# Scores on 64 rows: odd elements of q and k placed beside the even ones by SBUF to SBUF copies, and an earlier request of the values that are summed in fours

## The chip, the cores and the metric

The kernel runs on one core of a Trainium2 chip. The metric is the device time of one execution in microseconds (us), read as the median of several runs. The profile is one execution taken by the hardware profiler; its span is some 2 us shorter than the device time, and its times count from the start of the span. TensorE is the matmul engine (PE in the profile; PEld is its weight load), VectorE is DVE, ScalarE is ACT, GpSimd is POOL, and SyncE is SP. SPq and POOLq are the DMA requests that those engines issue.

A run is called slow when it lies over 1.5% above the fastest run of the same kernel.

## The reference, cut to what matters

There are 8 batches, 8 heads, 576 positions and 64 elements per head. Every head gets two attentions, which are added: one over means of four positions (144 by 144), and one over neighbours less than four positions away. Then a feed-forward layer with two large matrices follows.

```python
q_d = q.reshape(B, H, 144, 4, D).mean(axis=3)        # k_d, v_d alike
out_up = repeat(softmax(q_d @ k_d.T / 8) @ v_d, 4)   # "pooled" part
mask = abs(pos[:, None] - pos[None, :]) < 4
out_local = softmax(where(mask, q @ k.T / 8, -1e9)) @ v
x = (out_up + out_local), laid out as 4608 tokens of 512
h = x @ w_in                                          # 512 -> 2048
out = (h * sigmoid(1.702 * h)) @ w_out                # 2048 -> 512
```

## The kernel before

The kernel works in nine groups of 512 tokens. Group g does the two large products of its tokens, 64 matmuls of 128x512 each, and the attention of batch g+1 is threaded between them at fixed steps: scores of the first half of the heads at step 13, of the second half at 33, the four products with the values (AV) at 42 to 53, transposes at 62 and 71. So the attention of batches 2 to 7, which the change touches, runs in groups 1 to 6. I call those six "the groups" below.

The kernel views two elements (bf16) that lie side by side as one 32-bit word and lets VectorE transpose the words (STREAM_TRANSPOSE in the profile, 1.24 to 1.25 us for 128x576 of them). By the kernel's indices, a head's 64 elements then lie on 32 partitions, an even and an odd one (index `a`) beside each other. So a score needs two matmuls of 32 rows each, one for `a = 0` and one for `a = 1`:

```python
def prep_1(name, b, qd):
    tt = work.tile([128, S, 2], BF16, name=f"{name}T{qd}", ..., bufs=1)
    t32 = tt.rearrange("p t a -> p (t a)").bitcast(FP32)
    nc.vector.transpose(out=t32..., in_=store[b, qd].bitcast(FP32)...)
    dst[b, qd] = tt

def scores(b, qd, barred=False):
    sp = [ps_tile(), ps_tile()]
    for i in range(5):
        for a in range(2):
            for par in range(2):
                for r in range(4):
                    rows = slice(32 * r, 32 * r + 32)
                    nc.tensor.matmul(
                        sp[r // 2][64 * par : 64 * par + 64, r % 2, 60 * i : 60 * i + 60],
                        lhsT=kT[b, qd][rows, k0 : k0 + 64, a],
                        rhs=qT[b, qd][rows, q0 : q0 + 60, a],
                        start=(a == 0 ...), stop=(a == 1 ...),
                        tile_position=(32 * r, 64 * par), ...)
```

`scores_d` does the same for the pooled scores, from `kdT` and `qdT`, which GpSimd makes in `pool_qk`. GpSimd takes its work in the order of the program, as its timeline below shows (103.98 to 122.06 us). The order per group is:

```python
        elif b < B:
            if b > 2:
                load_v4(b)               # SyncE requests v in fours
            prep_qk(b, 0)                # VectorE: transposes of the first half
            pool_qk(b, 0)                # GpSimd: kdT and qdT of the first half
            if b + 1 < B:
                for qd in range(NQ):
                    load_qk(b + 1, qd)   # GpSimd requests q, k of the next batch (4 DMAs)
            prep_v(b, nc.gpsimd)         # GpSimd: v to bf16
            if b + 1 < B:
                load_v(b + 1)
            prep_qk(b, 1)                # VectorE: transposes of the second half
            pool_qk(b, 1)                # GpSimd: kdT and qdT of the second half
            prep_v4(b, nc.gpsimd)        # GpSimd: sums of four values -> vd
```

AV multiplies first with `vb` (local part) and then with `vd` (pooled part), so it wants the last item of GpSimd's list.

The softmax here doesn't subtract the row's maximum and nothing guards it: scores larger than these inputs give would overflow.

## Time and profile before

| | before |
|---|---|
| device time, median of the first 3 runs | 331.39 us (331.34 to 332.75) |
| span of the profile | 329.5 us |
| TensorE busy, mean granted clock | 93%, 0.995 |
| matmuls in the trace | 4987 |
| time of one group (2 to 6) | 33.4 to 34.3 us, TensorE busy 32.5 to 32.8 us of it |

The page of the kernel before: the busy time of each engine, TensorE's granted clock in 40 slices (9 is 90% or more of full speed), and the engines' shares of the chain of work that ended last.

```profile
span 329.5 us, 11220 instructions
...
PE 308.0 (93%) x4987; PEld 157.9 (48%) x5043; DVE 130.2 (40%) x215; ACT 184.1 (56%) x322; POOL 138.9 (42%) x168
...
PEclk9997999999999999999999999999999999999999
...
PE 87%; issue 4%; SPq 3%; ACT 2%; DVE 2%; DMA 1%; DVEq 0%; ACTq 0%
```

TensorE is the bound: 87% of the chain is its own work, and its mean granted clock is 1.00 from 31 us on (0.94 before that).

The second of the six groups, by the view of windows. The columns are the stretch, its length, then each engine's busy time and instructions (PE, PEld, DVE, ACT, POOL), the TensorE clock, the DMA share and GB/s:

```profile
102.20:135.90 33.70, 32.79 (x595) 16.90 (x601) 16.33 (x25) 20.95 (x36) 17.52 (x19) 1.00 0.68 142
```

GpSimd in the same group, from the timeline (start, length, engine, line, operation, output and inputs, and in brackets the idle time before it and what ended it):

```profile
103.98 1.15 POOL L276 TENSOR_TENSOR pq<-kT 128x576 f32<-128x576 bf16 x1 [15.95 <-DVE kT L260]
...
105.83 1.15 POOL L276 TENSOR_TENSOR pq<-qT 128x576 f32<-128x576 bf16 x1
...
109.80 2.36 POOL L291 CAST vb<-vf 128x2560 bf16<-128x2560 f32 x1
...
113.97 1.15 POOL L276 TENSOR_TENSOR pq<-qT 128x576 f32<-128x576 bf16 x1
...
121.22 0.84 POOL L300 TENSOR_TENSOR vd<-v 112x256 bf16<-112x256 f32 x1
```

It starts when the first transpose is done and then has no gap until 122.06. TensorE in that stretch (`pa` and `pm` are its accumulators; `es` and `ed` are the exponentials of the local and the pooled scores):

```profile
113.50 0.84 PE L351 MATMUL pa<-qT,kT 32*64 32x60 bf16 x80
114.14 0.59 PE L370 MATMUL pa<-qdT,kdT 32*64 32x144 bf16 x24
114.66 2.76 PE L618 MATMUL pm<-xT,w_in_bf 128*128 128x512 bf16 x11
...
121.87 0.58 PE L370 MATMUL pa<-qdT,kdT 32*64 32x144 bf16 x24
...
124.43 0.35 PE L409 MATMUL pa<-vb,es 64*64 64x65 bf16 x20
124.61 0.32 PE L431 MATMUL pa<-vd,ed 48*64 48x65 bf16 x17
```

A score stage, 80 local and 24 pooled matmuls, takes from 113.50 to 114.66, 1.16 us. The pooled scores of the second half come at 121.87, and qdT was ready at 115.86. AV comes to `vd` at 124.61, and its ninth product with `vd`, at 124.68, is the first that needs the last sums. They were ready 2.6 us earlier. That 2.6 us is the slack that the change has to live with.

### The profile page before, as it was taken

Reading aid. Unit: us, or ns where it says so; the run is one execution under the profiler, and the core shown is the slowest. Engines: PE = TensorE matmul, PEld = TensorE weight load, DVE = VectorE, ACT = ScalarE, POOL = GpSimd, SP = SyncE. Lnnn points to the kernel's source line nnn. Section 1 sums busy time; section 2 is a strip of 40 time slices with the busy share of each in tenths; the row PEclk is TensorE's granted clock in tenths of the full one; section 3 lists DMA queues with packets and bytes.
Section 4 is the critical chain, followed back from the end, with each engine's and each line's share of the span. In section 5 each row is a group of like instructions: output and inputs, shape, how many; then the busy total and the mean of one; then the engine's idle time right before and its main releaser. Section 6 shows DMA issues by size and latency. Waiting matters only on the chain.

```text
span 329.5 us, 11220 instructions
## 1 busy us (share of the span) xinstructions
PE 308.0 (93%) x4987; PEld 157.9 (48%) x5043; DVE 130.2 (40%) x215; ACT 184.1 (56%) x322; POOL 138.9 (42%) x168
## 2 busy tenths in 40 slices
PE   8767999789999999999999999998999999999995
PEld 3444455445554455455544555455444544444444
DVE  4870512770468036802771277225730560000000
ACT  2552773375936683667367746674566646415611
POOL 7890844049603970298029901990098000000000
PEclk9997999999999999999999999999999999999999
DMA  7999979999814991398339922993180110011011
GB/s 126 184 188 208 171 151 183 196 210 236 191 39 132 205 207 39 116 193 171 102 100 200 200 83 86 196 195 105 40 172 2 60 41 32 2 72 56 2 62 65
DMA packets 63552, 41.36 MB, mean 126 GB/s; under 512 B 44048, under 2 KB 54416, under 8 KB 63504
## 3 DMA queue, kind: packets, MB, share of 16 engines
q1 hardware_dynamic: 55056, 26.95, 35.8%
q0 software_dynamic: 8304, 13.63, 23.9%
q8 instruction: 39, 0.64, 0.9%
q14 instruction: 9, 0.07, 0.1%
q10 hardware_dynamic: 144, 0.07, 0.1%
HBM read 44.83 MB, written 9.44 MB: 165 GB/s over the span
## 4 chain that ended last, share of the span: by engine, by line
PE 87%; issue 4%; SPq 3%; ACT 2%; DVE 2%; DMA 1%; DVEq 0%; ACTq 0%
PE pm L618 35%; PE pm L674 33%; PE pa L351 3%; SPq L214 3%; PE pa L618 2%; PE pa L431 2%; PE pa L409 2%; PE pa L370 2%; PE pa L458 2%; PE pa L674 2%; DMA vf<-in_v_dram 1%; PE pm L689 1%; PE pa L484 1%; ACT vd L321 0%; PE pa L312 0%
## 5 line engine op out<-in xcount | busy, mean ns | idle before, releaser
L618 PE MATMUL pm<-xT,w_in_bf 128*128 128x512 bf16 x528 | 120.3, 380 | 1.4 <-DVE xT L561 0.7
L674 PE MATMUL pm<-w_out_bf,gT 128*128 128x512 bf16 x493 | 114.1, 379 | 5.4 <-issue 5.2
L629 ACT ACTIVATE gT<-pm 128x512 bf16<-128x512 f32 x136 | 81.0, 598 | 45.2 <-PE pm L618 45.2
L618 PEld LDWEIGHTS <-w_in_bf 128*128 128x128 bf16 x576 | 55.8, 98 | 68.4 <-issue 2.5
L674 PEld LDWEIGHTS <-gT 128*128 128x128 bf16 x560 | 51.7, 98 | 59.5 <-issue 0.2
L276 POOL TENSOR_TENSOR pq<-kT 128x576 f32<-128x576 bf16 x16 | 18.5, 1157 | 105.0 <-DVE kT L260 96.1
L395 DVE TENSOR_TENSOR es<-es,mask 128x600 bf16<-128x600 bf16 x28 | 20.6, 749 | 92.0 <-ACT es L381 91.2
L659 ACT ACTIVATE osb<-pm 128x512 f32<-128x512 f32 (+2 forms) x35 | 20.7, 592 | 40.2 <-PE pm L674 36.1
L534 ACT COPY od<-pa 128x384 f32<-128x384 f32 (+1 forms) x56 | 18.4, 412 | 32.4 <-DVE y L444 18.7
L444 DVE TENSOR_TENSOR y<-pa,rc 128x896 bf16<-128x896 f32 x32 | 34.9, 1092 | 1.1
L555 DVE TENSOR_TENSOR xT<-pa,od 128x570 bf16<-128x570 f32 x28 | 21.1, 753 | 12.0 <-ACT od L534 11.9
L381 ACT ACTIVATE es<-pa 128x600 bf16<-128x600 f32 x32 | 19.8, 668 | 7.0 <-PE pa L351 6.8
L297 POOL TENSOR_TENSOR v<-v 112x512 f32<-112x512 f32 x18 | 22.8, 1265 | 0.0
L661 DVE TENSOR_SCALAR osb<-pm 128x128 f32<-128x128 f32 x1 | 0.3, 292 | 55.3 <-ACT osb L659 55.3
L260 DVE STREAM_TRANSPOSE kT<-kb 128x576 f32<-128x576 f32 x16 | 20.0, 1249 | 2.0 <-DMA kb<-in_k_dram 2.0
L260 DVE STREAM_TRANSPOSE qT<-qb 128x576 f32<-128x576 f32 x16 | 19.8, 1239 | 0.9 <-DMA qb<-in_q_dram 0.7
L276 POOL TENSOR_TENSOR pq<-qT 128x576 f32<-128x576 bf16 x16 | 18.4, 1148 | 0.0
L291 POOL CAST vb<-vf 128x2560 bf16<-128x2560 f32 (+1 forms) x11 | 17.6, 1618 | 0.0
L442 DVE RECIPROCAL rc<-pa 128x14 f32<-128x14 f32 x32 | 7.7, 240 | 21.7 <-PE pa L431 21.7
L351 PE MATMUL pa<-qT,kT 32*64 32x60 bf16 x1280 | 14.0, 203 | 1.5 <-issue 1.5
L351 PEld LDWEIGHTS <-kT 32*64 32x64 bf16 x1280 | 11.8, 104 | 6.7 <-issue 5.5
L300 POOL TENSOR_TENSOR vd<-v 112x256 bf16<-112x256 f32 x18 | 13.7, 759 | 1.4
(90 smaller groups left out, 247.0 us busy)
## 6 DMA issues: line engine op xcount, KB each, us to landing
vf<-in_v_dram SPq DMA_DIRECT2D x80, 128.0 KB, 4.7
out_dram<-osb SPq DMA_DIRECT2D x35, 256.0 KB, 2.1
v<-in_v_dram SPq DMA_DIRECT2D x36, 192.0 KB, 6.1
kb<-in_k_dram POOLq DMA_DIRECT2D x16, 288.0 KB, 6.8
qb<-in_q_dram POOLq DMA_DIRECT2D x16, 288.0 KB, 7.1
w_out_bf<-in_moe_w_out_dram POOLq DMA_DIRECT2D x4, 512.0 KB, 12.1
w_in_bf<-in_moe_w_in_dram POOLq DMA_DIRECT2D x2, 512.0 KB, 5.7
w_in_bf<-in_moe_w_in_dram POOLq DMA_DIRECT2D x1, 1024.0 KB, 10.7
```

What stands on the lines that cost most here:

```text
L260: nc.vector.transpose(out=t32.rearrange("p (i c) -> p c i", c=18), in_=store[b, qd].bitcast(FP32).rearrange("p (c d) -> p c d", c=18),)
L276: nc.gpsimd.tensor_tensor(out=t1, in0=sv[:, :, 0:2, :], in1=sv[:, :, 2:4, :], op=ALU.add)
L297: eng.tensor_tensor(out=t1[0:112], in0=x[:, :, 0:2, :], in1=x[:, :, 2:4, :], op=ALU.add)
L351: nc.tensor.matmul(sp[r // 2][64 * par : 64 * par + 64, r % 2, 60 * i : 60 * i + 60], lhsT=kT[b, qd][rows, k0 : k0 + 64, a], rhs=qT[b, qd] ...
L381: nc.scalar.activation(out=es[2 * qd + u][:, :, 0:300], in_=sp[u][:, :, 0:300], func=AF.Exp, scale=inv_sqrt_d,)
L395: nc.vector.tensor_tensor(out=ev, in0=ev, in1=mask, op=ALU.mult)
L444: nc.vector.tensor_tensor(out=y, in0=ov[:, :, :, 0:D], in1=rc.to_broadcast([128, 2, 7, D]), op=ALU.mult,)
L555: eng.tensor_tensor(out=sub(xT[hp], t0 + 3, (57, 2), (114, 5), (1, 57)), in0=sub(x, 3, (509, 2), (57, 5), (1, 57)), in1=sub(od, 3, (57, 2) ...
L618: nc.tensor.matmul(acc, lhsT=w_in_bf[:, dmc, ffc * 128 : (ffc + 1) * 128], rhs=xT[dmc][:, g * TG : g * TG + TG], start=(dmc == 0), stop=(d ...
L629: nc.scalar.activation(out=gT[:, ffc, :], in_=acc, func=AF.Silu, scale=GELU_SCALE)
L659: eng.activation(out=osb, in_=ap, func=AF.Copy, scale=1.0 / GELU_SCALE)
L674: nc.tensor.matmul(ops[t], lhsT=gT[:, ffc, t * 128 : (t + 1) * 128], rhs=w_out_bf[:, ffc, :], start=(ffc == 0), stop=(ffc == n_ffc - 1),)
```

## The change

The intent is fewer score matmuls. A second transpose puts the same words into a second plane of the tile. Four copies per tile then shift the odd elements by one element into the neighbouring 32 partitions, so that one plane `j` holds all 64 elements of two heads on 64 partitions each. A score is then one matmul of 64 rows, and 208 matmuls per batch become 104. The copies are DMAs from SBUF to SBUF on SyncE's queue, 16 per batch. Batches 0 and 1 keep the old form. A second, small part requests the values that are summed in fours earlier: in the middle of the group before (step 34) instead of at the start of the group. Two smaller edits come along: the second half's transposes, and so its copies, now stand in front of the v loads on SyncE's queue, and GpSimd's scratch tile `pq` has one buffer instead of two (not in the cut below).

```diff
+    ROWS64 = 2
...
     def prep_1(name, b, qd):
-        tt = work.tile([128, S, 2], BF16, ..., bufs=1)
-        t32 = tt.rearrange("p t a -> p (t a)").bitcast(FP32)
-        nc.vector.transpose(...)
-        dst[b, qd] = tt
+        n = 2 if b >= ROWS64 else 1
+        tt = work.tile([128, 2, S, 2], BF16, ..., bufs=1)
+        for x in range(n):
+            t32 = tt[:, x].rearrange("p t a -> p (t a)").bitcast(FP32)
+            nc.vector.transpose(...)
+        if n == 2:
+            for x in range(2):
+                f = tt[:, x].rearrange("p t a -> p (t a)")
+                for r in range(2):
+                    src = 64 * r + 32 * x
+                    to = 64 * r + 32 * (1 - x)
+                    nc.sync.dma_start(
+                        out=f[to : to + 32, 0 : 2 * S - 1], in_=f[src : src + 32, 1 : 2 * S]
+                    )
+        dst[b, qd] = tt if n == 2 else tt[:, 0]
...
     def pool_qk(b, qd, names="kq"):
+            if b >= ROWS64:      # the same additions on tt[..., 0] of both planes,
+                ...              # into kdP and qdT with the planes apart
...
     def scores(b, qd, barred=False):
+        if b >= ROWS64:
+            for j in range(2):
+                for i in range(5):
+                    for par in range(2):
+                        for u in range(2):
+                            rows = slice(64 * u, 64 * u + 64)
+                            nc.tensor.matmul(
+                                sp[u][64 * par : 64 * par + 64, j, 60 * i : 60 * i + 60],
+                                lhsT=kT[b, qd][rows, j, k0 : k0 + 64, 0],
+                                rhs=qT[b, qd][rows, j, q0 : q0 + 60, 0],
+                                start=True, stop=True, tile_position=(64 * u, 64 * par))
+            return sp
...              # scores_d alike, 12 matmuls in place of 24
+    V4 = 34
...
-            if b > 2:
-                load_v4(b)
             prep_qk(b, 0)
             pool_qk(b, 0)
             if b + 1 < B:
                 for qd in range(NQ):
                     load_qk(b + 1, qd)
             prep_v(b, nc.gpsimd)
+            prep_qk(b, 1)
             if b + 1 < B:
                 load_v(b + 1)
-            prep_qk(b, 1)
             pool_qk(b, 1)
             prep_v4(b, nc.gpsimd)
...
+            if g and b + 1 < B:
+                steps.setdefault(V4, []).append(lambda b=b: load_v4(b + 1))
```

More of the change, by code (lines that the diff above doesn't have):

```diff
@@ L66 @@
     kdT = [persist.tile([128, 160, 2], BF16, name=f"kdT{i}") for i in range(NQ)]
+    kdP = [persist.tile([128, 2, 160], BF16, name=f"kdP{i}") for i in range(NQ)]
     PA = [psum.tile([128, 2, 512], FP32, name=f"pa{i}") for i in range(3)]
@@ L124, in fill @@
             nc.vector.memset(t[:, SD:160, :], 0.0)
+        for t in kdP:
+            nc.vector.memset(t[:, :, SD:160], 0.0)
         for t in vbs:
@@ L257, in prep_1 @@
         store, dst = {"k": (kf, kT), "q": (qf, qT)}[name]
-        tt = work.tile([128, S, 2], BF16, name=f"{name}T{qd}", tag=f"{name}T{qd}", bufs=1)
-        t32 = tt.rearrange("p t a -> p (t a)").bitcast(FP32)
-        nc.vector.transpose(
-            out=t32.rearrange("p (i c) -> p c i", c=18),
-            in_=store[b, qd].bitcast(FP32).rearrange("p (c d) -> p c d", c=18),
-        )
-        dst[b, qd] = tt
+        n = 2 if b >= ROWS64 else 1
+        tt = work.tile([128, 2, S, 2], BF16, name=f"{name}T{qd}", tag=f"{name}T{qd}", bufs=1)
+        for x in range(n):
+            t32 = tt[:, x].rearrange("p t a -> p (t a)").bitcast(FP32)
+            nc.vector.transpose(
+                out=t32.rearrange("p (i c) -> p c i", c=18),
+                in_=store[b, qd].bitcast(FP32).rearrange("p (c d) -> p c d", c=18),
+            )
[7 more added lines that the diff above has]
+                        out=f[to : to + 32, 0 : 2 * S - 1], in_=f[src : src + 32, 1 : 2 * S]
+                    )
+        dst[b, qd] = tt if n == 2 else tt[:, 0]
     def prep_qk(b, qd):
@@ L273, in pool_qk @@
                 continue
+            if b >= ROWS64:
+                sv = src[b, qd].rearrange("p x (j f) a -> p (x j) f a", f=4)[:, :, :, 0]
+                t1 = work.tile([128, 2 * SD, 2], FP32, name="pq", tag="pq", bufs=1)
+                nc.gpsimd.tensor_tensor(
+                    out=t1, in0=sv[:, :, 0:2], in1=sv[:, :, 2:4], op=ALU.add
+                )
+                if name == "k":
+                    dst = kdP[qd][:, :, 0:SD]
+                else:
+                    dst = work.tile([128, 2, SD], BF16, name=f"qdT{qd}", tag=f"qdT{qd}", bufs=1)
+                    qdT[b, qd] = dst
+                t1 = t1.rearrange("p (x j) f -> p x j f", x=2)
+                nc.gpsimd.tensor_tensor(
+                    out=dst, in0=t1[:, :, :, 0], in1=t1[:, :, :, 1], op=ALU.add
+                )
+                continue
             sv = src[b, qd].rearrange("p (j f) a -> p j f a", f=4)
-            t1 = work.tile([128, SD, 2, 2], FP32, name="pq", tag="pq")
+            t1 = work.tile([128, SD, 2, 2], FP32, name="pq", tag="pq", bufs=1)
             nc.gpsimd.tensor_tensor(
@@ L341, in scores @@
         sp = [ps_tile(), ps_tile()]
+        if b >= ROWS64:
[4 more added lines that the diff above has]
+                            rows = slice(64 * u, 64 * u + 64)
+                            k0 = 114 * i + KSTART[par]
+                            q0 = 114 * i + QSTART[par]
+                            nc.tensor.matmul(
+                                sp[u][64 * par : 64 * par + 64, j, 60 * i : 60 * i + 60],
+                                lhsT=kT[b, qd][rows, j, k0 : k0 + 64, 0],
+                                rhs=qT[b, qd][rows, j, q0 : q0 + 60, 0],
+                                start=True, stop=True,
+                                tile_position=(64 * u, 64 * par),
+                            )
+            return sp
         if barred:
@@ L363, in scores_d @@
         sd = sd or ps_tile()
+        if b >= ROWS64:
+            for kc in range(3):
+                for j in range(2):
+                    for u in range(2):
+                        rows = slice(64 * u, 64 * u + 64)
+                        nc.tensor.matmul(
+                            sd[64 * j : 64 * j + 64, u, SD * kc : SD * kc + SD],
+                            lhsT=kdP[qd][rows, j, 48 * kc : 48 * kc + 64],
+                            rhs=qdT[b, qd][rows, j, :],
+                            start=True, stop=True,
+                            tile_position=(64 * u, 64 * j),
+                        )
+            return sd
         bank = sd if sd is PM else [sd[:, u, :] for u in range(2)]
```

## The prediction

> **What bounds the kernel.** TensorE. The summary has it busy 93% of 329.5 us at clock 1.00, and the chain that ended last is 87% TensorE. From batch 2 on, groups repeat every 33.4 to 34.0 us (windows by group: TensorE 32.5 to 32.8 us busy). Only TensorE work, or a new TensorE wait, changes the time.
>
> **Removed.** Two 32-row score matmuls become one of 64 rows. Per batch: 160 local plus 48 pooled matmuls become 80 plus 24; over six batches 624 fewer. The chain charges 80 local matmuls 0.77 to 0.90 us (about 10 ns each) and 24 pooled ones 0.39 to 0.57 us. AV and transposes, which already run as 64-row tiles, take about 14 ns each (20 in 0.28 us). So 40 local should take about 0.55 us; 12 pooled with 144 columns about 0.22 us. That saves about 0.45 us per score stage, 0.9 us per batch, 5.4 us in all: not half of the scores' time[...].[...]
>
> **Added.** VectorE: four more transposes per batch, 1.09 us apart, run where it then idles 13 us (timeline). SyncE: 16 SBUF to SBUF copies of 74 KB per batch (stores of 128 KB and more occupy its queue 0.33 us each; estimate 0.3 each). GpSimd: the same additions, but its first waits for two transposes instead of one and then for a copy. [...]in this trace output stores land in 1.6 to 2.1 us.
>
> **Does it reach the critical path? I think yes, through GpSimd's order.** Before (third group): k transpose ends 103.91, GpSimd starts 103.98, works without a gap through pooling, load requests, v cast and sums of four, and ends at 122.06; AV wants the last sums at about 124.85. Slack 2.7 to 2.8 us in five groups, 5 us in the last. After: the q pooling of the first half can start only at 107.16 (fourth transpose) plus two copy issues (0.6) plus landing (about 1.7), about 109.5, instead of 105.83: 3.6 us later[...]. AV also comes 0.9 us sooner. So TensorE waits about 2 us for the sums in the middle of AV in each of five groups. Net: 5 x 2.0 minus 5.4 is about +4.6 us; I shade this down. The earlier v4 request relieves no wait: GpSimd did not wait for it before.
>
> **Predicted: 334.5 us** (before 331.39), 8 in 10 within 328 to 341. Chances: faster by over 2% 0.03, within 2% 0.77, slower by over 2% 0.20.
>
> **What would show it.** Right: TensorE matmul count down by 624; score stages near 0.75 us instead of 1.2; transposes doubled; GpSimd ending 3 to 4 us later within the group; in the TensorE timeline, a wait of 1.5 to 3 us for GpSimd's vd sums between the local and down parts of the first AV of a group; the groups' period near 34.5 us. Wrong: no wait there, period near 32.8 us, total near 326. Also wrong: a wait before the scores themselves (copies landing over 4 us late), total above 340.
>
> **What would make it wrong.** The landing time of the copies, which no record of before shows; each 1 us there is worth about 5 us.

Passages that no trace or run of this case shows are cut from it. Three of them carried no term of the sum: a reason for the price of the 64-row matmuls, the bracket behind it, and a clause about landing times. The fourth was a term, about 0.3 us for extra semaphore waits. The sum was, per group: the q pooling 3.6 us later, plus the 0.3, plus 0.9 for AV coming sooner, less 2.7 to 2.8 of slack, is about 2.0 us of waiting (about 1.75 without the term). Five groups of 2.0 minus the 5.4 saved is +4.6 on 331.39, or 336.0, shaded down to 334.5. The 1.7 us for the landing can be held against the stores in the trace before, which landed in 1.6 to 2.1 us in the median, by size (the longest took 4.4).

## The result, and the profile after

The changed kernel takes 368.87 us (median of 4 runs, 367.38 to 370.1) beside 332.07 us of the kernel before (4 runs, 331.34 to 333.16). The ratio is 1.110, with a 95% interval of 1.104 to 1.117: slower by 11%. A ratio here is always the mean time of one kernel's fast runs over that of the other's fast runs of the same rounds, so it is not quite the ratio of the medians. The prediction of 334.5 us was wrong, and so was its range of 328 to 341.

The page of the changed kernel, the same lines, and the DMA issues that are new (bytes each, median us from issue to landing):

```profile
span 365.9 us, 10241 instructions
...
PE 312.7 (85%) x4363; PEld 156.0 (43%) x4419; DVE 160.7 (44%) x241; ACT 184.0 (50%) x322; POOL 141.4 (39%) x168
...
PEclk9898999998989999999899989999899989999999
...
PE 41%; DVE 15%; POOL 15%; DMA 11%; issue 8%; SPq 5%; ACT 3%; DVEq 1%; POOLq 0%; ACTq 0%
...
kT<-kT SPq DMA_DIRECT2D x48, 71.9 KB, 2.1
qT<-qT SPq DMA_DIRECT2D x48, 71.9 KB, 2.1
```

TensorE has 624 matmuls fewer, exactly as planned, and yet it was busy 4.7 us longer, because its clock now dips: 0.963 in the mean beside 0.995, and the 493 large matmuls with `w_out` in the trace take 394 ns each beside 379. The chain of waits goes through VectorE, GpSimd and the copies: TensorE is no longer the bound by itself.

The six groups took 203.4 us before (35.1, 33.7, 33.5, 33.4, 34.3, 33.4) and take 239.2 us after (45.5, 37.6, 39.3, 40.8, 38.8, 37.2). Their difference of 35.8 us is nearly all of the span's 36.4 us. The first two of them, by windows:

```profile
67.70:113.20 45.50, 35.69 (x491) 17.50 (x497) 20.72 (x31) 21.83 (x39) 17.80 (x19) 0.92 0.88 178
113.20:150.80 37.60, 31.89 (x490) 16.03 (x496) 20.53 (x29) 20.95 (x36) 17.80 (x19) 1.00 0.72 159
```

The second group, at full clock, shows the gain that was hoped for: 31.89 us of TensorE work instead of 32.79. But the group is 3.9 us longer. TensorE in it, from the timeline:

```profile
124.49 0.52 PE L381 MATMUL pa<-qT,kT 64*64 64x60 bf16 x40
124.83 0.36 PE L416 MATMUL pa<-qdT,kdP 64*64 64x144 bf16 x12
125.13 2.76 PE L678 MATMUL pm<-xT,w_in_bf 128*128 128x512 bf16 x11
...
133.38 0.38 PE L416 MATMUL pa<-qdT,kdP 64*64 64x144 bf16 x12 [1.37 <-POOL qdT L301]
...
135.74 0.35 PE L469 MATMUL pa<-vb,es 64*64 64x65 bf16 x20
135.93 0.20 PE L491 MATMUL pa<-vd,ed 48*64 48x65 bf16 x4
137.77 0.22 PE L491 MATMUL pa<-vd,ed 48*64 48x65 bf16 x4 [1.64 <-POOL vd L331]
139.79 0.28 PE L491 MATMUL pa<-vd,ed 48*64 48x65 bf16 x10 [1.80 <-POOL vd L331]
```

The score stage takes from 124.49 to 125.13, 0.64 us in place of 1.16. Then come three waits, all for GpSimd: one for qdT in front of the pooled scores of the second half, two for the sums of four in the middle of AV. Over the whole kernel the view of waits sums them (engine, tile and line, what it waited for: us in total, times, longest):

```profile
PE pa L491 <- POOL vd L331: 19.8, 12, 1.8
...
PE pa L416 <- POOL qdT L301: 7.8, 5, 1.9
```

A sixth wait at the same matmuls, of 0.9 us in the fifth group, is put down to ScalarE, which came last there by the profile; I count it with the five, 8.7 us.

Why GpSimd is late is read from its own timeline in that group:

```profile
119.24 1.15 POOL L292 TENSOR_TENSOR pq<-kT 128x576 f32<-128x576 bf16 x1 [18.59 <-DMA kT<-kT]
...
121.82 1.15 POOL L292 TENSOR_TENSOR pq<-qT 128x576 f32<-128x576 bf16 x1 [0.69 <-DMA qT<-qT]
...
125.78 2.36 POOL L322 CAST vb<-vf 128x2560 bf16<-128x2560 f32 x1
...
131.44 1.15 POOL L292 TENSOR_TENSOR pq<-qT 128x576 f32<-128x576 bf16 x1 [1.45 <-DMA qT<-qT]
...
139.01 0.73 POOL L331 TENSOR_TENSOR vd<-v 112x256 bf16<-112x256 f32 x1
```

Counted from the start of the group (113.2, and 102.2 before), the q pooling of the first half starts at 8.62 us instead of 3.63, which is 4.99 us late. The second wait for a copy adds 1.45. The last sums end at 26.54 us instead of 19.86, which is 6.7 us late; the slack was 2.6.

And why the copies are late is read from SyncE's queue in the timeline (here x4 with the time of all four), and from the view of the copies' line for 112 to 135 us (durations of one issue in ns, minimum, median, maximum; then the time to landing):

```profile
115.15 2.49 SPq L276 DMA_DIRECT2D kT<-kT  x4
117.73 2.44 SPq L276 DMA_DIRECT2D qT<-qT  x4
120.27 2.43 SPq L276 DMA_DIRECT2D kT<-kT  x4
122.79 2.45 SPq L276 DMA_DIRECT2D qT<-qT  x4
```

```profile
L276 SPq DMA_DIRECT2D kT<-kT x8: 529/581/587, 115.1 to 122.1; - x8
L276 SPq DMA_DIRECT2D qT<-qT x8: 541/561/590, 117.7 to 124.7; - x8
...
DMA to landing us min/median/max: 2.0/2.1/6.6
```

One issue takes 0.53 to 0.59 us. From one group of four to the next it is 2.52 to 2.58 us, so a copy takes SyncE about 0.64 us with the gaps. The sixteen run from 115.15 to 125.24, 10.1 us, longer than the eight transposes that feed them (8.8 us, from 113.83 to 122.64). Most copies land 2.0 to 2.1 us after the start of their issue (the trace has the landing of 12 of the 16). The last two q copies, issued at 124.06 and 124.65, took 4.64 and 6.63 us. GpSimd had requested q and k of the next batch, 288 KB each, between 123.65 and 125.82, so these two were on their way beside them; e_loads_last below tests whether that is the cause. The third to fifth groups show the same (last two copies 4.6 to 6.3 us). In the sixth, which requests no q and k, the second half's copies all land in 2.0 to 2.1.

The last part is the clock. Six stretches of 3.4 us at half clock lie in the groups, starting at 83.3, 100.4, 178.9, 216.5, 257.4 and 295.0; the kernel before has none after 31 us. Two windows of TensorE alone, the first with no such stretch behind it and the second with one (columns: stretch, length, busy time and matmuls, clock, DMA share, GB/s):

```profile
134.50:137.90 3.40, 1.76 (x35) 1.00 0.86 185
...
213.10:216.50 3.40, 0.22 (x4) 0.99 1.14 236
```

The two waits of the fourth group, 1.65 and 1.80 us, fall into one such window, which leaves 0.22 us of work in it, and the next 3.4 us run at half clock:

```profile
216.50:219.90 3.40, 2.83 (x57) 1.70 (x58) 2.58 (x4) 0.00 (x0) 0.18 (x1) 0.50 1.10 209
```

The second group has practically the same two waits, but the boundary between two windows (137.9) falls between them, and no half clock follows. The clock's records in the traces of the two kernels hold two values only, 1.0 and 0.5. But for the last record of each, cut off by the end, every stretch at 0.5 lasts 3.413 us, and those at 1.0 between them last whole multiples of it, 3 to 22 times in the changed kernel and 88 times (300.4 us) before. So the six starts lie on one grid, 5, 28, 39, 51 and 62 steps of 3.413 us behind the first. I laid that grid over the trace of the changed kernel and took, for each step, the share of time in which some matmul ran: the five lowest steps after 60 us (0.07 to 0.30) are all followed by half clock, of two at 0.43 one is, and none from 0.52 up. The longest idle stretch tells less: in the steps below 0.6 it is 1.5 to 1.8 us where half clock followed and 1.4 to 1.8 where it did not. The grid does not start with the kernel: stretches begin at 27.27 us before and at 28.73 after, which is no whole number of steps apart.

The sum, as an estimate worked out from these numbers: waits of TensorE over 0.3 us in the groups rose from 1.1 to 32.2 us (19.8 for `vd`, 8.7 for qdT, the rest copies and issue), +31.1. The scores save about 0.5 us per stage, 12 stages, about -6. Six stretches of 3.41 us at half clock cost at most 1.7 us each, up to +10. Together up to +35, against the +35.8 measured.

### The profile page after: what moved, and what is told of

Read it like the earlier page. It is cut to its first block, busy times and chain, and to the rows that moved or that the text cites. A ratio compares the mean times of both kernels' runs of the same rounds, so it can differ in the third digit from the quotient of the medians.

```text
span 365.9 us, 10241 instructions
## 1 busy us (share of the span) xinstructions
PE 312.7 (85%) x4363; PEld 156.0 (43%) x4419; DVE 160.7 (44%) x241; ACT 184.0 (50%) x322; POOL 141.4 (39%) x168
## 3 DMA queue, kind: packets, MB, share of 16 engines
q0 software_dynamic: 8304, 13.63, 21.8%
## 4 chain that ended last, share of the span: by engine, by line
PE 41%; DVE 15%; POOL 15%; DMA 11%; issue 8%; SPq 5%; ACT 3%; DVEq 1%; POOLq 0%; ACTq 0%
PE pm L734 17%; PE pm L678 12%; DMA qT<-qT 9%; POOL v L328 6%; SPq L276 5%; DVE xT L615 5%; DVE qT L266 4%; DVE kT L266 4%; POOL vd L331 4%; POOL pq L292 3%; PE pa L678 2%; PE pa L491 2%; DMA qb<-in_q_dram 2%; DVE y L504 2%; ACT od L594 1%
## 5 line engine op out<-in xcount | busy, mean ns | idle before, releaser
L734 PE MATMUL pm<-w_out_bf,gT 128*128 128x512 bf16 x493 | 120.5, 394 | 7.5 <-issue 7.3
L734 PEld LDWEIGHTS <-gT 128*128 128x128 bf16 x560 | 53.3, 101 | 66.1 <-issue 10.6
L292 POOL TENSOR_TENSOR pq<-kT 128x576 f32<-128x576 bf16 x12 | 13.9, 1160 | 120.6 <-DMA kT<-kT 83.4
L455 DVE TENSOR_TENSOR es<-es,mask 128x600 bf16<-128x600 bf16 x28 | 24.5, 897 | 68.6 <-ACT es L441 68.1
L266 DVE STREAM_TRANSPOSE kT<-kb 128x576 f32<-128x576 f32 x28 | 32.9, 1243 | 2.8 <-DMA kb<-in_k_dram 2.2
L266 DVE STREAM_TRANSPOSE qT<-qb 128x576 f32<-128x576 f32 x28 | 32.8, 1238 | 0.8 <-DMA qb<-in_q_dram 0.7
L491 PE MATMUL pa<-vd,ed 48*64 48x65 bf16 x640 | 14.4, 201 | 20.3 <-POOL vd L331 19.8
L491 PEld LDWEIGHTS <-ed 48*64 48x64 bf16 x640 | 11.0, 111 | 21.7 <-issue 21.7
L292 POOL TENSOR_TENSOR pq<-qT 128x576 f32<-128x576 bf16 x12 | 14.3, 1196 | 10.7 <-DMA qT<-qT 9.4
L447 ACT ACTIVATE ed<-pa 128x864 bf16<-128x864 f32 x15 | 13.5, 899 | 2.0 <-PE pa L416 2.0
```

What stands on the lines that cost most here:

```text
L266: nc.vector.transpose(out=t32.rearrange("p (i c) -> p c i", c=18), in_=store[b, qd].bitcast(FP32).rearrange("p (c d) -> p c d", c=18),)
L292: nc.gpsimd.tensor_tensor(out=t1, in0=sv[:, :, 0:2], in1=sv[:, :, 2:4], op=ALU.add)
L455: nc.vector.tensor_tensor(out=ev, in0=ev, in1=mask, op=ALU.mult)
L491: nc.tensor.matmul(o[64 * pos : 64 * pos + 64, j, c0 : c0 + 65], lhsT=Ed[64 * j : 64 * j + 48, u, q0 : q0 + 64], rhs=vd[64 * j : 64 * j + ...
L734: nc.tensor.matmul(ops[t], lhsT=gT[:, ffc, t * 128 : (t + 1) * 128], rhs=w_out_bf[:, ffc, :], start=(ffc == 0), stop=(ffc == n_ffc - 1),)
```

## The experiments

My theory (A) after the result: the copies make GpSimd late, by A1 the slow issue on SyncE and A2 landing beside the q and k requests; because GpSimd works in order, its sums of four come late, TensorE waits, and the clock halves. Rivals: (B) something on TensorE or the added transposes and strided reads is itself slow; (C) the copies' traffic or SyncE's time harms other DMAs, whoever waits for them; (D) the earlier request of the values does the harm. The times are medians of all runs, slow ones included. Except for e_split, which was one look, each was timed in several rounds beside the kernel before.

| run | us (range) | ratio to before (95%) | periods of the six groups |
|---|---|---|---|
| changed kernel | 368.87 (367.38-370.1) | 1.110 (1.104-1.117) | 45.5, 37.6, 39.3, 40.8, 38.8, 37.2 |
| e_nocopy (wrong) | 329.54 (327.19-332.88) | 0.988 (0.981-0.995) | 35.2, 34.2, 34.3, 32.9, 33.5, 32.5 |
| e_unread | 336.88 (333.68-339.69) | 1.009 (1.002-1.016) | 39.7, 34.0, 33.4, 35.0, 34.2, 33.5 |
| e_loads_last | 349.74 (346.66-355.63) | 1.048 (1.041-1.055) | 41.4, 37.2, 34.6, 38.5, 36.1, 37.1 |
| e_sums_first | 335.91 (335.55-337.19) | 1.010 (1.006-1.015) | 38.9, 33.8, 34.0, 34.3, 34.2, 32.5 |
| e_both | 339.92 (335.79-343.48) | 1.013 (1.006-1.020) | 40.3, 33.5, 36.2, 34.1, 34.5, 32.5 |
| e_v4only | 334.73 (334.39-335.23) | 1.006 (1.002-1.010) | 36.3, 34.0, 33.4, 35.5, 34.0, 33.4 |
| e_v4back | 386.16 (383.24-389.7) | 1.158 (1.150-1.166) | 44.8, 43.5, 41.9, 43.0, 42.5, 39.0 |
| e_split | 421.11 (1 run) | one run, state unknown | 51.2, 48.3, 47.7, 48.6, 47.6, 46.5 |
| e_best | 339.5 (332.53-341.49) | profile slow | 41.5, 32.6, 34.8, 34.7, 34.2, 32.5 |
| e_quiet (wrong) | 329.22 (328.98-330.45) | 0.995 (0.989-1.001) | 37.1, 32.5, 33.2, 32.5, 32.5, 32.5 |
| e_best2 | 333.98 (330.74-334.96) | 1.002 (0.998-1.007) | 39.2, 32.6, 32.5, 34.3, 34.5, 32.8 |

### e_nocopy: the change without its copies

The odd elements are never moved, so half of the products are wrong; everything else is the changed kernel. (The comparison with the reference still passed, probably because the inputs have a scale of 0.1, so that the weights are nearly uniform and the tolerance does not see this error. The numbers are wrong all the same, and a passed comparison says little about the copies of the other variants.)

```diff
-        if n == 2:
-            for x in range(2):
-                ...
-                    nc.sync.dma_start(out=f[to : to + 32, ...], in_=f[src : src + 32, ...])
         dst[b, qd] = tt if n == 2 else tt[:, 0]
```

> The changed kernel without its SBUF to SBUF copies (wrong result on purpose; transposes, 64-row matmuls, layouts and order stay). Theory A (the copies arrive late, GpSimd's order passes that on, TensorE waits for its sums): no TensorE wait for vd or qdT, clock 1.00, groups near 32.7 us, about 326 us in all. Rival B (the 64-row matmuls, the doubled transposes or GpSimd's strided reads are themselves slow): over 345 us.

Measured: 329.54 us, ratio 0.988. The wait for `vd` shrinks to 0.2 or 0.3 us, as here in the second group (timeline of TensorE), and there is no half clock in the groups (mean over the span 0.993):

```profile
124.68 0.28 PE L482 MATMUL pa<-vd,ed 48*64 48x65 bf16 x10 [0.22 <-POOL vd L322]
```

So the copies, and what follows from them, cause the whole loss; the 64-row matmuls, the doubled transposes and the strided reads are not slow. B is refuted. It also sets a ceiling: with copies that cost nothing, the change is worth 1.2%. The second transposes alone do use up slack: the sums of the second group end 21.8 us after its start, 1.9 later than before. The fast runs, 327.2 to 331.0 us, all lie above the expected 326; four unexplained "issue" stalls of TensorE (idle time for which the profile shows nothing that it waited for), 1.07, 1.11, 1.18 and 0.39 us, stand in the groups, of which the kernel before has one of 0.62. I come back to them.

### e_unread: all the added traffic, but nobody reads it

The scores stay on 32 rows. The second transpose writes into a tile of its own, and the same 16 copies go into another one that nobody reads.

```diff
-    ROWS64 = 2
+    ROWS64 = 99
...
+        tiles = [tt]
+        if b >= 2:
+            tiles.append(work.tile([128, S, 2], BF16, name=f"{name}U", ...))
-        for x in range(n):
+        for t in tiles:
             nc.vector.transpose(...)
...
+            un = work.tile([128, S, 2], BF16, name=f"{name}W", ...)
+            fo = un.rearrange("p t a -> p (t a)")
-                        out=f[to : to + 32, ...], in_=f[src : src + 32, ...]
+                        out=fo[to : to + 32, ...], in_=f[src : src + 32, ...]   # f: view of tiles[x]
...
-        dst[b, qd] = tt if n == 2 else tt[:, 0]
+        dst[b, qd] = tt
```

> The 32-row scores of before in the changed kernel's order, with the second transpose and all 16 copies per batch still made, but into tiles that nobody reads. Theory A: about 332 us, since nothing waits for the copies. Rival C (SyncE's time and the DMA traffic of the copies slow loads and stores and so the kernel): over 340 us.

Measured: 336.88 us, ratio 1.009. The loss sits in the first of the groups (39.7 us). There a transpose of the second half was late, q pooling waited 4.38 us for it, TensorE waited 0.58 and 2.02 us for `vd`, and one half-clock stretch followed (mean clock of the run 0.985). The other five groups take 33.4 to 35.0 us. By the fast runs (333.7 to 337.7 us) the traffic, the added transposes and SyncE's time cost 0.9% in all, about 3 us, more than A's number and below C's: C is refuted as the main cause. What costs is that somebody waits for the copies.

### e_loads_last: q and k of the next batch requested behind the sums of four

```diff
             pool_qk(b, 0)
-            if b + 1 < B:
-                for qd in range(NQ):
-                    load_qk(b + 1, qd)
             prep_v(b, nc.gpsimd)
...
             prep_v4(b, nc.gpsimd)
+            if b + 1 < B:
+                for qd in range(NQ):
+                    load_qk(b + 1, qd)
```

> The changed kernel with GpSimd's q/k load requests of the next batch moved behind its sums of four. Theory A with its part A2 (the last q copies land in 4.6 to 6.6 us instead of 2.1 because those loads share the DMA engines): all copies land in about 2.1 us, the wait for qdT in the second score stage is gone, the waits for vd fall from 3.4 to below 1 us per group, groups near 33.3 us, 331 to 338 us in all. Without A2 (only SyncE's issue rate makes them late): the last copies still take over 4 us, over 350 us in all.

Measured: 349.74 us, ratio 1.048; the profiled run itself, of span 353.9 us, was a slow one, so the periods in the table are those of a slow run. The copies' line for the third group (148 to 166 us), and the waits:

```profile
DMA to landing us min/median/max: 2.0/2.1/2.7
```

```profile
PE pa L491 <- POOL vd L331: 9.7, 7, 2.0
...
PE pa L416 <- POOL qdT L301: 1.9, 1, 1.9
```

With the requests gone from beside them, the copies of this group land in 2.0 to 2.7 us (the longest from the second group on takes 3.3), and the wait for qdT is gone from the second group on. That confirms A2. But the time missed the expected 331 to 338 by far: 9.7 us of waits for `vd` remain in the profiled run, because AV now also comes earlier, by the 1.4 us that the qdT wait had held it up, and because the sums still stand at the end of GpSimd's list. Stretches at half clock follow several of them (mean clock 0.952 in that run), and issue stalls of 0.48 to 2.65 us stand in the groups too.

### e_sums_first: the sums of four in front of the pooling

GpSimd idles before the first copies land (18.59 us in the timeline above, from the end of the last group's sums). The sums wait only for the values in fours, which the changed kernel requests a group ahead, and not for the copies, so they are put into that idle time.

```diff
         elif b < B:
+            prep_v4(b, nc.gpsimd)
             prep_qk(b, 0)
...
             pool_qk(b, 1)
-            prep_v4(b, nc.gpsimd)
```

> The changed kernel with GpSimd's sums of four moved in front of its pooling, where it idles. Theory A: no TensorE wait for vd in any group, the wait of about 1.4 us for qdT stays, the half-clock stretches are fewer, groups near 34 us, 334 to 342 us. Rival B: over 350 us.

Measured: 335.91 us, ratio 1.010, as expected. No wait for `vd` over 0.3 us is left; the wait for qdT stays, 1.36 us in a typical group, and one half-clock stretch in the first group (mean clock of the run 0.990):

```profile
PE pa L416 <- POOL qdT L301: 8.9, 6, 2.3
```

This one moved call takes back 33 of the 37 us. It shows that the order in GpSimd's queue, not the lateness of the pooled keys and queries as such, is what turned late copies into most of the lost time.

### e_both: both moves

```diff
+            prep_v4(b, nc.gpsimd)
             prep_qk(b, 0)
             pool_qk(b, 0)
-            if b + 1 < B: (the load_qk loop)
             prep_v(b, nc.gpsimd)
...
             pool_qk(b, 1)
-            prep_v4(b, nc.gpsimd)
+            if b + 1 < B: (the load_qk loop)
```

> The changed kernel with both moves: GpSimd's sums of four in front of its pooling and its q/k load requests behind the pooling of the second half. Theory A: no TensorE wait for vd or qdT from the second group on, copies landing in about 2.1 us there, groups near 33 us, 327 to 332 us in all, at or below before. If the 64-row scores cost more than they save (rival B), it stays above 336 us.

Measured: 339.92 us (335.79 to 343.48; the three fast runs 335.8 to 338.1), ratio 1.013: the expectation failed. By its own words a time above 336 us would speak for B, but e_nocopy (0.988) and e_quiet below (0.995) have the same 64-row scores. After the first group there is no wait for `vd` or qdT left, so A has nothing more to explain; but five stalls that the profile calls "issue" stand in the groups, 1.16, 0.77, 1.92, 1.37 and 1.83 us, 7.05 in all. That is a fourth term, and it was not in the theory.

### e_v4only and e_v4back: the second part of the change alone, and undone

e_v4only is the kernel before with only the earlier request; e_v4back is the changed kernel without it.

```diff
# e_v4only, against the kernel before
+    V4 = 34
-            if b > 2:
-                load_v4(b)
+            if g and b + 1 < B:
+                steps.setdefault(V4, []).append(lambda b=b: load_v4(b + 1))
# e_v4back, against the changed kernel
+            if b > 2:
+                load_v4(b)
-            if g and b + 1 < B:
-                steps.setdefault(V4, []).append(lambda b=b: load_v4(b + 1))
```

> The kernel before with nothing but the earlier request of the sums-of-four values (behind step 34 of the group before). I expect no change, 330 to 334 us: GpSimd did not wait for these loads. Rival: this move is itself what slows, over 340 us.

> The changed kernel with the sums-of-four values requested at the group's start again, in front of the copies on SyncE's queue. Theory A: six more issues of about 0.45 us and their traffic stand ahead of the copies, so these are about 3 us later; 375 to 400 us. If the earlier request was harmful: below 362 us.

Measured: e_v4only 334.73 us, ratio 1.006; e_v4back 386.16 us, 1.158. Alone, the earlier request gains nothing; it costs 0.6%, just outside the expected 330 to 334 us, with issue stalls of 1.51, 1.82 and 0.34 us. Within the change it is worth about 16 us by the fast runs: without it the six requests of 192 KB go out at the start of the group, on the same queue in front of the copies. So D is refuted: this part of the change helps the other part.

### e_split: each copy as two of half the size

```diff
-                    nc.sync.dma_start(
-                        out=f[to : to + 32, ...], in_=f[src : src + 32, ...]
-                    )
+                    for h in (0, 16):
+                        nc.sync.dma_start(
+                            out=f[to + h : to + h + 16, ...], in_=f[src + h : src + h + 16, ...]
+                        )
```

> The changed kernel with every copy issued as two of 16 partitions: the same bytes, 32 issues per batch instead of 16. If an issue costs SyncE a fixed 0.5 to 0.6 us, the last q copy starts about 9 us later and groups lengthen by 6 to 10 us: 400 to 430 us. If the issue time goes with the bytes or the descriptors, an issue takes about 0.3 us and the total stays near 368 us.

Measured: 421.11 us in one run. The copies' line in the second group:

```profile
L277 SPq DMA_DIRECT2D kT<-kT x16: 522/587/1327, 123.2 to 138.5; - x16
L277 SPq DMA_DIRECT2D qT<-qT x16: 507/587/594, 128.3 to 144.3; - x16
```

Half the bytes, and an issue still takes 587 ns in the median (561 to 581 in the changed kernel). For these copies the cost of an issue does not go with the bytes, and 32 of them keep SyncE for 21.7 us instead of 10.1. The groups are 6 to 11 us longer still. This confirms A1: the count of the copies on one queue, not their bytes, sets when the last one lands.

### e_best and e_best2: an order that should get the gain

Both put the sums first, the v cast behind the first pooling (it fills the time in which the second half's copies are on their way), and the q and k requests behind that; and both leave batch 2 on 32 rows (`ROWS64 = 3`), since the first group always suffered. In e_best2 batch 2 also keeps its sums last.

```diff
-    ROWS64 = 2
+    ROWS64 = 3
...
+            if b > 2:                    # in e_best for every b
+                prep_v4(b, nc.gpsimd)
             prep_qk(b, 0)
             pool_qk(b, 0)
+            prep_v(b, nc.gpsimd)
             if b + 1 < B: (the load_qk loop)
-            prep_v(b, nc.gpsimd)
             prep_qk(b, 1)
...
             pool_qk(b, 1)
-            prep_v4(b, nc.gpsimd)
+            if b == 2:                   # not in e_best
+                prep_v4(b, nc.gpsimd)
```

> Sums of four first, then GpSimd's order: pooling of the first half, v cast, q/k load requests, pooling of the second half; 64-row scores from batch 3 on instead of batch 2 (the first group has late loads and stores beside the copies in every variant). Expected: no wait for vd or qdT from the second group on, first group back to about 35 us, 330 to 334 us in all, so level with before within 1%. If the waits for qdT come back (the loads still meet the last copies): 336 us or more.

> As the last variant (64-row scores from batch 3 on; pooling of the first half, v cast, q/k load requests, pooling of the second half), but batch 2 keeps its sums of four last, since in the first group they waited for their loads. Expected: first group near 35 us, later groups 32.5 us[...], 329 to 334 us in all: level with before, and not more than 1% faster.

Measured: e_best 339.5 us over six runs, of which five count as slow beside its fastest (332.53), among them the profiled one. Its first group takes 41.5 us, in part because the sums, and the pooling behind them, waited there until 72.27 us for v, which is still on its way from the kernel's start. e_best2 takes 333.98 us, ratio 1.002: level with the kernel before. Its second and third groups are what one wanted:

```profile
106.20:138.70 32.50, 31.60 (x490) 15.77 (x496) 19.95 (x29) 20.84 (x36) 11.75 (x13) 1.00 0.74 157
```

That is 1.2 us less than the 33.7 us of the second group before. But the first group still takes 39.2 us, with an issue stall of 2.66 us and a half-clock stretch behind it (mean clock of the run 0.985), and the fourth and fifth have 34.3 and 34.5 us, with waits of 0.9 and 1.0 us in front of the pooled scores and issue stalls of 0.72 and 0.89. (A term is cut from its expectation: 0.5 to 2 us in the later groups for such stalls, under a name for their cause that no run shows. So "32.5 us" stood for 33 to 34.5.) No version I ran that computes the right result beats the kernel before.

### e_quiet: e_both without the bulk loads

To see whether the issue stalls come from bulk loads, q, k and the values in fours are not loaded from batch 3 on; the old ones are used again. (The other form of v is still loaded.) The result is wrong (relative error 0.123).

```diff
     def load_qk(b, qd):
+        if b > 2:
+            kf[b, qd], qf[b, qd] = kf[2, qd], qf[2, qd]
+            return
...
     def load_v4(b):
+        if b > 2:
+            return
```

> The variant with both moves (339.9 us), but without the q/k loads and the sums-of-four loads from batch 3 on (old data is used again, wrong result on purpose; copies, v loads and stores stay). Its remaining TensorE waits were of the kind issue, 0.8 to 1.9 us each, 7 us in all, each about 1 us after a 16 KB packet of the instruction queue. [...]they fall below 2 us in groups two to six and the total below 333 us. If traffic has nothing to do with them, they stay near 7 us and the total above 336 us.

(The condition in front of "they fall below 2 us" is cut, since it named a cause that no run shows; what stays of it is that the stalls come from the bulk loads.)

Measured: 329.22 us, ratio 0.995. From the second group on, one issue stall of 0.56 us is left of the 5.9 in e_both:

```profile
105.10:137.60 32.50, 32.50 (x498) 15.80 (x497) 21.88 (x29) 20.84 (x36) 16.00 (x15) 1.00 0.43 111
```

(There is no gap left. In the line of e_best2 above, the records of some 8 of the 128 large matmuls are missing, in this one none.) So the stalls need the bulk loads, which one profile of each shows. What exactly is slow in them is not shown. The stalls over 0.3 us of e_nocopy, e_both, e_quiet and e_v4only, 13 in the groups, start 0.3 to 2.5 us after the start of a transfer of 16 KB on the DMA queue that the profile calls "instruction", and end 2.2 to 2.9 us after that start, whatever their length. The stall of 0.62 us in the kernel before and the one of 1.52 us in the changed kernel fit: they start 1.9 and 1.3 us after such a start and end 2.5 and 2.8 us after it. On that queue the page counts 39 packets and 0.64 MB before and 34 and 0.56 MB after, one per 257 or 258 of TensorE's counted instructions. No run moved these transfers themselves, so whether they tie the stalls to the loads stays open. The changed kernel has few such stalls (one of 1.52 us in the groups), perhaps since it waits for other things first.

## Why the prediction was wrong, point by point

Right in the prediction:

- "TensorE matmul count down by 624": 4987 to 4363. "Score stages near 0.75 us": 0.64. The saving of 5.4 us was about 6 in the trace. The price behind it, 14 ns a matmul in place of 10, is not borne out: from start to start a local matmul took 8.4 ns beside 8.0 before, a pooled one 12 to 15 beside 16. The 10 and 14 ns were shares of the chain divided by the count, 0.77 us for 80 and 0.28 us for 20: both are about 8 ns each plus 0.12 to 0.13 us once, and from start to start the AV matmuls, too, took 8.3. A first-half stage takes 0.55 of its old time and not half because the 0.15 us from the start of its last matmul to the next large one stay.
- The mechanism: "a wait ... for GpSimd's vd sums between the local and down parts of the first AV of a group". It is there in every group, and e_sums_first shows that it is GpSimd's order that makes it.
- "The earlier v4 request relieves no wait": e_v4only gains nothing alone. That it keeps six requests out of the copies' way, worth 16 us within the change (e_v4back), the prediction did not see.
- The transposes are harmless as long as nothing else is late: e_nocopy keeps them and is 1.2% faster.

Wrong, by step:

1. "Plus two copy issues (0.6)", an estimate of 0.3 us each taken from stores of 128 KB and more. A copy's issue took 0.53 to 0.59 us, at a pace of 0.64, and all earlier copies stand in the same queue. The fourth transpose of the second group ended at 118.32, and the last q copy of the first half was issued only at 119.59, 1.3 us later, and landed at 121.66: 3.34 us in place of the 2.3 that I had put. The term was mis-sized because I took the duration of another kind of DMA and counted only the last two copies; e_split shows that it is a cost per issue and not per byte (587 ns in the median for half the bytes). The profile before already held longer issues on the same queue: 0.64 us (median) for the 80 v loads of 128 KB, 0.43 for the loads of the values in fours.
2. "Landing (about 1.7)": a free copy took 2.06 us from the start of its issue, 1.5 from its end, so that was about right. But the last copies of the second half, beside the q and k requests, took 4.6 to 6.6 us. Here a step was missing: I costed the copies as if nothing else were on the DMA engines, and looked only at the first half. e_loads_last shows the cause.
3. "3.6 us later", and the 0.3: the sums ended 6.7 us later, 4.99 from the first half, 1.45 from the second, and some 0.25 from slower operations beside them.
4. "So TensorE waits about 2 us for the sums in each of five groups": 10 us. The waits for `vd` were 19.8 us, 3.3 per group and in the sixth group too (0.87 and 1.80), and those for qdT in front of the pooled scores of the second half, which I had not looked at, another 8.7. Against the text's sign for being wrong, "a wait before the scores themselves", no such wait above 0.35 us appeared; the total went above 340 all the same.
5. The clock was missing altogether. Ten microseconds of added waits were in my prediction, and I treated them as if TensorE came back at full speed. Six stretches at half clock cost up to 10 us more (an estimate).

Put together, the net "5 x 2.0 minus 5.4" was really about 31 + 10 - 6. My last sentence named the weak point, the landing time, as worth "about 5" per microsecond; it was worth more, since the second half's copies, a second wait and the clock hung on it.

## What to carry to other kernels

Cost a set of small DMAs by pace times count on the queue that issues them, and by their landing beside the traffic that is there at that moment, not by one free DMA: here 0.64 us times 16, and 4.6 to 6.6 us to landing in place of 2.1. On an engine that takes its work in order, as GpSimd does here, look at what stands behind an item that becomes late: here one moved call, which put independent sums in front of the late pooling, took back 33 of 37 us. And compare the ceiling first: with free copies the change was worth 1.2%, too little to pay for any new wait on the engine that bounds the kernel.
